# Values two slots behind their gates, and chain steps spread over the slots

## The chip, the cores and the metric

One core of a Trainium2 chip runs the whole program. The metric is the device time of one execution in microseconds (us). A profiled execution also has a span: the time from its first to its last instruction.

## The reference

The program is an attention block over 32 learned points, and then a gated feed-forward block. x has 4 batches of 12,416 tokens with 128 channels.

```
h   = softmax(scale * I @ x.T) @ x      # 32 x 128 for each batch
y   = softmax(scale * x @ h.T) @ h      # 12,416 x 128 for each batch
out = (relu(y @ w_gate) * (y @ w_val)) @ w_out
```

w_gate and w_val are 128 x 1,536, w_out is 1,536 x 128. Outputs are fp32.

## The kernel before, in words

y is never formed. h @ w_gate and h @ w_val are 32 x 1,536 and are kept as `hgv`, four blocks of 32 partitions (gate, value, gate, value). With p2, the unnormalised exponentials of the second softmax, a gate is p2 times a block of hgv: a matmul over 32 rows only. Gates and values for two blocks of 512 tokens use four different row groups of the TensorE array, so the four matmuls can run side by side. Both are off by the softmax sum, so the output is scaled by the square of its reciprocal at the end (z2i, twice in L498).

The main loop (L606 to L655) goes through slots. A pair is two blocks of 512 tokens; it has 12 slots, one for each 128 of the 1,536 columns. A batch has 12 pairs and then three small slots for the last 128 tokens: 147 slots, 588 in all. In a slot:

- TensorE forms the unit's two gates (L591, tile g_ps, one PSUM bank each, three banks with the tag "g") and, for the unit of the slot before, two values (v_ps, a tile of two banks, two tiles). The order is first gate, both values, second gate (L623 to L625).
- ScalarE writes Relu of the gates to g16 (L648, three buffers).
- VectorE multiplies g16 of the slot before with its values into gv (L651). This is the "multiply".
- TensorE does steps of jobs. A chain is 12 matmuls with w_out that add into the one "o" bank (L481), one for each slot of a pair; a pair has two chains, k = 0 and 1. ScalarE evicts a finished chain to oT (L487); a DMA on SyncE's queue transposes it; GpSimd scales it (L498); a DMA stores it. Other jobs: the softmax sums (z2, eight small matmuls for every second pair, then a reciprocal on VectorE), and in each of the first three batches the sums over tokens for the next batch's h (h_part, join).
- TensorE does fills: scores for the next pair (`ev_s2`, L164) and scores for the next batch (`s1`, L367). Each takes one of the three "g" banks, and ScalarE exponentiates it one slot later (L174; L377, tile p1T). hgv for the next batch is filled the same way (L143, L153).

`post[at]` holds work for other engines that is placed at the start of slot `at`: evictions, casts, transposes, loads, stores. The schedule is manual, so the order in the code is the order on each engine, and each engine works through its queue in that order.

Jobs go first come, first served. Each slot has a budget of 3; a chain step costs 1 and may run from its own slot on (`first + i`). When a job is done, the next may start two slots later (`free = at + 2`). Fills stand at fixed slots.

The next batch's x is loaded, cast on GpSimd, transposed by a DMA (L353, slot 16q + 11 of the batch) and scored (slot 16q + 20) while the present batch runs.

Of the kernel before, what the change touches and what calls it, by code (L numbers as in the profile page):

```python
# [2 lines left out]

# [7 lines left out]
FP16 = mybir.dt.float16  # L11
AF = mybir.ActivationFunctionType
ALU = mybir.AluOpType
# [4 lines left out]
def kernel(  # L18
# [133 lines left out]
    def hgv_evac(hgv, ps, k):  # L152
        nc.scalar.copy(out=hgv[:, k * BLK : (k + 1) * BLK], in_=ps)  # L153
# [117 lines left out]
    def slot(b, pr, s):  # L271
        return b * SPB + pr * NFF + s

    fill = defaultdict(list)
    post = defaultdict(list)

    def ev_s2(b, pr, at):
        def pe():
            s = state[b]
            ps = s2_pe(s["hT"], s["xT"], pr)  # L280

            def act():
                p2s[(b, pr)] = s2_exp(ps, pr)

            post[at + 1].append(act)

        fill[at].append(pe)

    jobs = []

    def job(steps, evac):
        jobs.append(dict(steps=steps, evac=evac))

    def ev_z2(b, pr):
        def pe():
            if pr < NPAIR:
                box["ps"] = z2_pe([p2s[(b, pr)], p2s[(b, pr + 1)]])
            else:  # L300
                box["ps"] = z2_rest_pe(p2s[(b, pr)])

        def dve(at):
            if pr < NPAIR:
                z2i = st([P, 2, TPB, 2], FP32, "z2i", 3)
                nc.vector.reciprocal(out=z2i, in_=box["ps"])
                z2is[(b, pr)] = z2i[:, 0, :, :]
                z2is[(b, pr + 1)] = z2i[:, 1, :, :]
            else:
                z2i = st([P, 1, 1], FP32, "z2r", 2)  # L310
                nc.vector.reciprocal(out=z2i[:, 0, :], in_=box["ps"])
                z2is[(b, pr)] = z2i

        box = {}
        base = slot(b, pr, 0)
        job([(base + (6 if pr < NPAIR else 0), 3, pe)], dve)

    for b in range(B):
        for pr in range(NPAIR + 1):
            if (b, pr) == (0, 0):  # L320
                pass
            elif pr == 0:
                ev_s2(b, 0, slot(b - 1, NPAIR - 1, 8))
            else:
                ev_s2(b, pr, slot(b, pr - 1, 3))


    def plan_phase1(b):
# [11 lines left out]
        for q in range(NCH):  # L340
            t0, t1 = crange(q)

            def load(q=q):
                s["x32", q] = load_x(b, q)

            def cast(q=q, t0=t0, t1=t1):
                nc.gpsimd.tensor_copy(  # L347
                    out=s["x16"][:, t0:t1, :], in_=s["x32", q]
                )

            def transp(q=q, t0=t0, t1=t1):
                s["xT"][q] = new_xT(q)
                nc.sync.dma_start_transpose(  # L353
                    out=s["xT"][q],
                    in_=s["x16"][:, t0:t1, :].rearrange("p t c -> p (t c)"),
                )

            at = at0 + 16 * q
            post[at + 3].append(load)
            post[at + 7].append(cast)  # L360
            post[at + 11].append(transp)

            def s1(q=q, at=at + 20):
                ps = bank("g", "s1T_ps")
                for r in range(4):
                    t = q * CT + r * TPB
                    nc.tensor.matmul(  # L367
                        ps[32 * r : 32 * r + 32, :],
                        indT,
                        xTs(s["xT"], t, TPB),  # L370
                        start=True,
                        stop=True,
                    )

                def act():
                    p1T = st([P, BLK], FP16, "p1T", 2)
                    nc.scalar.activation(  # L377
                        out=p1T, in_=ps, func=AF.Exp, scale=sm_scale, accum_out=s["zp"][:, q : q + 1]
                    )

                    def tr():
                        p1g = st([P, TPB, P], FP16, "p1g", NQ)
                        nc.sync.dma_start_transpose(out=p1g, in_=p1T)
                        s["p1g"][q] = p1g

                    post[at + 2].append(tr)

                post[at + 1].append(act)

            if q < NQ:  # L390
                fill[at + 20].append(s1)

        at = at0 + 16 * NQ + 16

        def s1_rest(at=at):
            ps = bank("g", "s1T_ps")
            nc.tensor.matmul(ps[0:M, 0:P], indT, xTs(s["xT"], NT - 1, 1), start=True, stop=True)

            def act():
                p1T = st([P, BLK], FP16, "p1T", 2)  # L400
                nc.scalar.activation(
                    out=p1T[0:M, 0:P],
                    in_=ps[0:M, 0:P],
                    func=AF.Exp,
                    scale=sm_scale,
                    accum_out=s["zp"][0:M, NQ : NQ + 1],
                )

                def tr():
                    p1r = st([P, 1, M], FP16, "p1r", 1)  # L410
                    nc.sync.dma_start_transpose(out=p1r, in_=p1T[0:M, 0:P])
                    s["p1r"] = p1r

                post[at + 2].append(tr)

            post[at + 1].append(act)

        fill[at].append(s1_rest)

        def h_part(q):  # L420
            if q == 0:
# [31 lines left out]
        def finish(at):  # L453
            s["hT"] = finish_h(s["hz_ps"][:, 0, :], s["hz_ps"][:, 1, :])
            s["hgv"] = new_hgv()
            for k in range(3):

                def mk(k=k, a=at + 2 + 2 * k):
                    ps = hgv_pe(s["hT"], k)
                    post[a + 1].append(lambda: hgv_evac(s["hgv"], ps, k))  # L460

                fill[at + 2 + 2 * k].append(mk)

        at = at0 + 16 * NQ + 19
        s["jobs"] = [
            ([(at, 2, lambda q=q: h_part(q)) for q in range(NQ + 1)], sums),
            ([(at, 2, join)], finish),
        ]

    for b in range(1, B):  # L470
# [3 lines left out]
    def chain(w, gv, key, k, t0, first):  # L474
# [10 lines left out]
        def evac(at):  # L485
# [29 lines left out]

            post[at + 1].append(tr)

        per = 1 if w == BLK else 4
        job(
            [(first + (i // per), 1 if w == BLK else 0.5, lambda i=i: step(i)) for i in range(NFF)],  # L520
            evac,
        )

    def units():
        for b in range(B):
            for pr in range(NPAIR + 1):
                base = slot(b, pr, 0)
                p2, hgv = p2s[(b, pr)], state[b]["hgv"]  # L530
                if pr < NPAIR:
# [7 lines left out]
                    for k in range(2):  # L539
                        chain(  # L540
                            BLK,
                            lambda i, k=k, gv=gv: gv(i, k),
                            (b, pr),
                            k,
                            (2 * pr + k) * TPB,
                            base + 2,
                        )
                    if b + 1 < B and pr == 8:
                        for j in state[b + 1]["jobs"]:
# [19 lines left out]
                else:  # L569
                    gvr = st([P, NFF, P], FP16, "gvr", 1)  # L570
                    ev_z2(b, pr)
                    chain(P, lambda i, g=gvr: g[:, i, :], (b, pr), 0, NT - 1, base + 2)
                    for s in range(3):
                        yield dict(
                            mm=[
# [27 lines left out]

        return gate

    free = 0  # L606
    at = 0
    todo_units = units()
    before = None
    while True:  # L610
        unit = next(todo_units, None)
        if not (unit or before or fill or post or jobs):
            break

        gs = []
        if unit:
            gate = gate_banks(unit)
            gs = [(gate, m) for m in unit["mm"][0]]
        vs = []
        if before:  # L620
            before["v"] = bank("v", "v_ps", [P, 2 * BLK])
            vs = [(lambda *m, ps=before["v"]: form(ps, *m), m) for m in before["mm"][1]]
        h = (len(gs) + 1) // 2  # L623
        for f, m in gs[:h] + vs + gs[h:]:
            f(*m)  # L625
        for f in post.pop(at, []):
            f()
        budget = 3.0 if unit else 100.0
        while jobs and free <= at and budget > 0:
            j = jobs[0]  # L630
            when, cost, f = j["steps"][0]
            if when > at:
                break
            f()
            budget -= cost
            j["steps"].pop(0)
            if not j["steps"]:
                jobs.pop(0)
                free = at + 2
                post[at + 1].append(lambda at=at, j=j: j["evac"](at + 1))  # L640
        for f in fill.pop(at, []):
            f()

        if unit:
            n = unit["dst"].shape[-1]
            g16 = unit["g16"] = st([P, 2 * BLK], FP16, "g16", 3)
            for k, ps in enumerate(unit["g"]):
                nc.scalar.activation(out=g16[:, k * BLK : (k + 1) * BLK], in_=ps, func=AF.Relu)  # L648
        if before:
            n = before["dst"].shape[-1]  # L650
            nc.vector.tensor_tensor(  # L651
                out=before["dst"], in0=before["g16"][:, 0:n], in1=before["v"][:, 0:n], op=ALU.mult
            )
        before = unit
        at += 1  # L655


# [28 lines left out]
```

## Time and profile before

| | |
|---|---|
| median of 3 runs | 806.71 us (802.96 to 806.79) |
| the profiled execution | 806.86 us, span 805.1 us, granted clock 0.901 |
| busy share of the span | TensorE 89%, ScalarE 88%, VectorE 87%, GpSimd 26% |
| VectorE multiplies (L651) | 576 of 128x1024, 674.4 us |
| ScalarE Relu (L648) | 616.3 us |
| chain matmuls (L481) | 354.0 us |

PE is TensorE's matmul row, PEld its weight loads, DVE VectorE, ACT ScalarE, POOL GpSimd, SP SyncE. Durations of neighbouring instructions can overlap by a part, so the distance from start to start says what one costs in a row of them. The granted clock is the share of full speed that TensorE was given. "Idle before <-X" names the instruction that ended an engine's idle time.

### The profile page before, as it was taken

How to read it: one execution, taken by the hardware profiler on the slowest of the kernel's cores; microseconds unless marked ns; L12 is line 12 of the kernel's file. 1: busy time of each engine (PE TensorE's matmuls, PEld its weight loads, DVE VectorE, ACT ScalarE, POOL GpSimd, SP SyncE). 2: the span in 40 equal slices, each digit the busy share in tenths (PEclk: the TensorE clock that was granted, in tenths of full speed). 3: DMA queues.
4: the chain of work that ended last, by engine and by line, in shares of the span. 5: the costliest groups of instructions: out<-in, count | busy, mean ns of one | idle time of the engine just before them, and what ended most of it. 6: DMA issues, size and time to landing. Idle time of an engine off the chain costs nothing.

```text
span 805.1 us, 13705 instructions
## 1 busy us (share of the span) xinstructions
PE 717.5 (89%) x4621; PEld 207.6 (26%) x4621; DVE 698.5 (87%) x666; ACT 707.2 (88%) x1390; POOL 207.6 (26%) x418
## 2 busy tenths in 40 slices
PE   5798898898999998989999999889899999998894
PEld 4422222222232222222222222222223222222221
DVE  3399999998998899899898988988899999898993
ACT  4589999998999899898898989998899999998993
POOL 0302332321232233322112333322122122212222
PEclk9779999998988899899897989998898899998998
DMA  8515555421154366441134547442112112121212
GB/s 312 185 24 144 125 144 149 137 55 35 50 149 127 106 146 155 114 96 55 27 103 132 143 102 168 112 122 54 35 50 71 43 46 73 47 60 40 59 54 63
DMA packets 121158, 78.76 MB, mean 98 GB/s; under 512 B 102880, under 2 KB 105472, under 8 KB 118016
## 3 DMA queue, kind: packets, MB, share of 16 engines
q1 hardware_dynamic: 121088, 77.89, 35.9%
q8 instruction: 36, 0.59, 0.3%
q14 instruction: 34, 0.28, 0.1%
HBM read 27.80 MB, written 25.43 MB: 66 GB/s over the span
## 4 chain that ended last, share of the span: by engine, by line
PE 56%; ACT 24%; issue 10%; DVE 8%; DMA 2%; POOL 0%; SPq 0%; POOLq 0%; ACTq 0%; DVEq 0%
PE o_ps L481 28%; PE g_ps L591 19%; ACT g L648 17%; DVE gv L651 8%; ACT oT L487 5%; PE v_ps L591 3%; PE s_ps L164 2%; DMA o<-oT 1%; PE xTb_ps L239 1%; DMA x<-in_x_dram 1%; PE h_ps L431 1%; PE hgv_ps L143 1%; ACT x L223 1%; PE s1T_ps L367 1%; ACT p L251 0%
## 5 line engine op out<-in xcount | busy, mean ns | idle before, releaser
L651 DVE TENSOR_TENSOR gv<-g,v_ps 128x1024 f16<-128x1024 f16 x576 | 674.4, 1214 | 68.7 <-PE g_ps L591 37.9
L648 ACT ACTIVATE g<-g_ps 128x512 f16<-128x512 f32 x1164 | 616.3, 621 | 45.2 <-PE g_ps L591 36.9
L481 PE MATMUL o_ps<-gv,wo 128*128 128x512 f16 x1152 | 354.0, 417 | 14.0 <-DVE gv L651 13.7
L591 PE MATMUL g_ps<-p,hgv 32*128 32x512 f16 (+1 forms) x1200 | 318.2, 401 | 41.8 <-ACT g L648 29.4
L498 POOL TENSOR_SCALAR osb<-o,z2i 128x128 f32<-128x128 f16 x384 | 166.2, 447 | 544.3 <-DMA o<-oT 361.5
L591 PE MATMUL v_ps<-p,hgv 32*128 32x512 f16 (+1 forms) x1200 | 245.2, 404 | 6.1 <-DVE gv L651 5.8
L591 PEld LDWEIGHTS <-hgv 32*128 32x128 f16 x2400 | 77.8, 92 | 281.0 <-issue 276.5
L481 PEld LDWEIGHTS <-wo 128*128 128x128 f16 x1200 | 90.3, 102 | 215.7 <-issue 176.8
L487 ACT CAST oT<-o_ps 128x512 f16<-128x512 f32 (+1 forms) x100 | 58.1, 581 | 4.0 <-PE o_ps L481 3.8
L174 ACT ACTIVATE p<-s_ps 128x512 f16<-128x512 f32 x48 | 29.1, 606 | 18.1 <-PE s_ps L164 16.0
L347 POOL CAST x<-x 128x2048 f16<-128x2048 f32 x18 | 34.0, 1889 | 10.7 <-DMA x<-in_x_dram 10.7
L164 PE MATMUL s_ps<-xT,hT 128*64 128x512 f16 x96 | 22.7, 468 | 2.1 <-DVE hT L137 1.6
L241 DVE COPY xT<-xT_ps 128x1024 f16<-128x1024 f16 x6 | 4.2, 692 | 14.5 <-PE xT_ps L239 14.5
L377 ACT ACTIVATE p1T<-s1T_ps 128x512 f16<-128x512 f32 x18 | 11.0, 614 | 2.8 <-PE s1T_ps L367 2.2
L164 PEld LDWEIGHTS <-hT 128*64 128x64 f16 x96 | 6.2, 112 | 25.9 <-issue 23.9
L243 ACT COPY xT<-xTb_ps 128x1024 f16<-128x1024 f16 x6 | 6.1, 1012 | 6.8 <-PE xTb_ps L239 6.8
L184 PEld LDWEIGHTS <-p 128*128 128x128 f16 x192 | 6.5, 97 | 21.4 <-issue 21.4
L239 PEld LDWEIGHTS <-x 128*128 128x128 f16 x97 | 9.1, 136 | 9.4 <-ACT x L223 5.3
L223 ACT CAST x<-x 128x1024 f16<-128x1024 f32 x6 | 6.2, 1038 | 4.3 <-DMA x<-in_x_dram 4.3
L239 PE MATMUL xT_ps<-eye,x 128*128 128x128 f16 x49 | 6.3, 305 | 3.9 <-DVE x L222 3.9
L153 ACT CAST hgv<-hgv_ps 128x512 f16<-128x512 f32 x12 | 6.9, 596 | 2.9 <-PE hgv_ps L143 2.7
L239 PE MATMUL xTb_ps<-eye,x 128*128 128x128 f16 x48 | 5.8, 295 | 4.1 <-ACT x L223 4.1
(75 smaller groups left out, 123.0 us busy)
## 6 DMA issues: line engine op xcount, KB each, us to landing
x<-in_x_dram SPq DMA_DIRECT2D x24, 1024.0 KB, 5.2
out_dram<-osb SPq DMA_DIRECT2D x96, 256.0 KB, 2.1
o<-oT SPq DMA_TRANSPOSE x100, 2.4
x<-in_moe_w_gate_dram SPq DMA_DIRECT2D x1, 768.0 KB, 4.0
x<-in_moe_w_val_dram SPq DMA_DIRECT2D x1, 768.0 KB, 4.3
x<-in_moe_w_out_dram SPq DMA_DIRECT2D x1, 768.0 KB, 5.9
xT<-x SPq DMA_TRANSPOSE x18, 4.3
p1g<-p1T SPq DMA_TRANSPOSE x18, 2.4
```

The source lines that it names most:

```text
L164: nc.tensor.matmul(ps[64 * k : 64 * k + 64, :], hT, xTs(xT, t0, TPB), start=True, stop=True)
L174: nc.scalar.activation(out=p2, in_=ps, func=AF.Exp, scale=sm_scale)
L223: nc.scalar.copy(out=x16[:, t0 + 8 : t1, :], in_=x32[:, 8:CT, :])
L239: nc.tensor.transpose(ps[:, t - a, :], x16[:, t, :], eye16)
L347: nc.gpsimd.tensor_copy(out=s["x16"][:, t0:t1, :], in_=s["x32", q])
L377: nc.scalar.activation(out=p1T, in_=ps, func=AF.Exp, scale=sm_scale, accum_out=s["zp"][:, q : q + 1])
L481: nc.tensor.matmul(c["ps"][:, 0:w], wo[:, i, :], gv(i), start=(i == 0), stop=(i == NFF - 1))
L487: nc.scalar.copy(out=oT[:, 0:w], in_=c["ps"][:, 0:w])
L498: nc.gpsimd.tensor_scalar(out=osb[:, t, :], in0=o16[:, t, :], scalar1=zz, scalar2=zz, op0=ALU.mult, op1=ALU.mult,)
L591: nc.tensor.matmul(ps[:, cols], hgv[:, s * P : (s + 1) * P], p2, start=True, stop=True)
L648: nc.scalar.activation(out=g16[:, k * BLK : (k + 1) * BLK], in_=ps, func=AF.Relu)
L651: nc.vector.tensor_tensor(out=before["dst"], in0=before["g16"][:, 0:n], in1=before["v"][:, 0:n], op=ALU.mult)
```

## The change

The jobs get a fixed number of steps for each of their slots, with one list for a job that starts on time and one for a job that starts late. The next job may start in the slot right after one ends. A chain of pair `base` starts from slot base + 10 (k = 0) and base + 16 (k = 1) on, not from base + 2. Fills get a first and a last slot; one fill is done in a slot without job steps, in a job's third slot, or when its last slot has come, and it stands ahead of the job's steps. Values are formed two slots behind their gates, ahead of both gates of the slot, and g16 has a fourth buffer.

```
+    def fill(first, last, f):
+        heapq.heappush(fills, (first, last, len(fills) + 1000 * first, f))
...
-        job([(base + (6 if pr < NPAIR else 0), 3, pe)], dve)
+        job([(base + (10 if pr < NPAIR else 0), pe)], dve, ([1], [1]))
...
-                ev_s2(b, 0, slot(b - 1, NPAIR - 1, 8))
+                a = slot(b - 1, NPAIR - 1, 0)
+                ev_s2(b, 0, a + 6, a + 11)
             else:
-                ev_s2(b, pr, slot(b, pr - 1, 3))
+                a = slot(b, pr - 1, 0)
+                ev_s2(b, pr, a + 1, a + (5 if pr == NPAIR else 8))
...
-                fill[at + 20].append(s1)
+                fill(at + 18, at + 26, s1)
...
-                fill[at + 2 + 2 * k].append(mk)
+                fill(at + 2, at + 7 + 3 * k, mk)
...
+            ([(at, lambda q=q: h_part(q)) for q in range(NQ + 1)], sums, ([1, 2, 2, 2],) * 2),
+            ([(at, join)], finish, ([1], [1])),
...
-        per = 1 if w == BLK else 4
-        job(
-            [(first + (i // per), 1 if w == BLK else 0.5, lambda i=i: step(i)) for i in range(NFF)],
-            evac,
-        )
+        if w == BLK:
+            steps = [(first if i == 0 else 0, lambda i=i: step(i)) for i in range(NFF)]
+            counts = ([1, 2, 1, 2, 3, 3], [1, 3, 2, 3, 3])
+        else:
+            steps = [(first + i // 4, lambda i=i: step(i)) for i in range(NFF)]
+            counts = ([4, 8], [4, 8])
+        job(steps, evac, counts)
...
-                            base + 2,
+                            base + 10 + 6 * k,
...
+    window = [None, None]
+    job_slot = 0
...
+        window.append(unit)
+        ready = window.pop(0)
...
+        if ready:
+            ready["v"] = bank("v", "v_ps", [P, 2 * BLK])
+            for m in ready["mm"][1]:
+                form(ready["v"], *m)
         if unit:
             gate = gate_banks(unit)
+            for m in unit["mm"][0]:
+                gate(*m)
...
+            if job_slot == 0 and j["steps"][0][0] <= at:
+                j["counts"] = j["counts"][1 if at > j["steps"][0][0] else 0]
+            if job_slot > 0 or j["steps"][0][0] <= at:
+                n_steps = j["counts"][job_slot] if job_slot < len(j["counts"]) else 3
+                job_slot += 1
+
+        if fills and fills[0][0] <= at:
+            if not n_steps or (job_slot == 3) or min(f[1] for f in fills) <= at:
+                heapq.heappop(fills)[3](at)
+        for _ in range(n_steps):
+            if j["steps"] and j["steps"][0][0] <= at:
+                j["steps"].pop(0)[1]()
...
-            g16 = unit["g16"] = st([P, 2 * BLK], FP16, "g16", 3)
+            g16 = unit["g16"] = st([P, 2 * BLK], FP16, "g16", 4)
...
-        if before:
-            n = before["dst"].shape[-1]
+        if ready:
+            n = ready["dst"].shape[-1]
             nc.vector.tensor_tensor(
-                out=before["dst"], in0=before["g16"][:, 0:n], in1=before["v"][:, 0:n], op=ALU.mult
+                out=ready["dst"], in0=ready["g16"][:, 0:n], in1=ready["v"][:, 0:n], op=ALU.mult
             )
```

## Rows read from the trace of the kernel before

**Rows 1.** The page's busy times, and the granted clock in 40 slices (tenths).

```profile
PE 717.5 (89%) x4621; PEld 207.6 (26%) x4621; DVE 698.5 (87%) x666; ACT 707.2 (88%) x1390; POOL 207.6 (26%) x418
...
PEclk9779999998988899899897989998898899998998
```

**Rows 2.** Busy time by stretch, the loop: all engines; then L651 alone (busy, count, clock).

```profile
38.80:792.60 753.80, 690.97 (x4284) 189.14 (x4283) 687.08 (x636) 686.35 (x1362) 196.16 (x399) 0.90 0.35 90
...
38.80:792.60 753.80, 682.00 (x588) 0.90 0.35 90
```

**Rows 3.** The waits of the whole execution: total us, times, longest us.

```profile
DVE gv L651 <- PE g_ps L591: 37.9, 92, 1.3
ACT g L648 <- PE g_ps L591: 36.9, 61, 1.1
PE g_ps L591 <- ACT g L648: 29.4, 86, 0.6
```

**Rows 4.** The timeline of TensorE's matmuls (start, us, instruction), half clock, then full.

```profile
301.32 0.60 PE L591 MATMUL g_ps<-p,hgv 32*128 32x512 f16 x1
...
303.26 0.60 PE L591 MATMUL g_ps<-p,hgv 32*128 32x512 f16 x1
...
309.93 0.39 PE L591 MATMUL g_ps<-p,hgv 32*128 32x512 f16 x1
...
310.26 0.82 PE L481 MATMUL o_ps<-gv,wo 128*128 128x512 f16 x3
311.01 0.38 PE L591 MATMUL g_ps<-p,hgv 32*128 32x512 f16 x1
```

**Rows 5.** The timeline of ScalarE, then of VectorE, from 311 us on.

```profile
311.43 1.09 ACT L648 ACTIVATE g<-g_ps 128x512 f16<-128x512 f32 x2
312.40 0.59 ACT L487 CAST oT<-o_ps 128x512 f16<-128x512 f32 x1
312.87 1.12 ACT L648 ACTIVATE g<-g_ps 128x512 f16<-128x512 f32 x2
313.83 0.65 ACT L377 ACTIVATE p1T<-s1T_ps 128x512 f16<-128x512 f32 x1
...
314.40 3.87 ACT L648 ACTIVATE g<-g_ps 128x512 f16<-128x512 f32 x7
...
315.63 3.48 DVE L651 TENSOR_TENSOR gv<-g,v_ps 128x1024 f16<-128x1024 f16 x3 [0.34 <-PE g_ps L591]
```

**Rows 6.** The timeline of VectorE: two runs of multiplies without a break.

```profile
41.03 4.60 DVE L651 TENSOR_TENSOR gv<-g,v_ps 128x1024 f16<-128x1024 f16 x4
...
88.86 13.98 DVE L651 TENSOR_TENSOR gv<-g,v_ps 128x1024 f16<-128x1024 f16 x12 [0.24 <-PE g_ps L591]
```

**Rows 7.** L651 by stretch: sums of the 25 half-clock, then 25 full-clock stretches.

```profile
sum 132.90, DVE 101.91; mean DVE 4.08
...
sum 590.70, DVE 552.29; mean DVE 22.09
```

**Rows 8.** Chain matmuls by stretch: 3 us before 25 falls; full clock otherwise.

```profile
sum 75.00, PE 7.55; mean PE 0.30
...
sum 503.20, PE 254.14; mean PE 10.17
```

**Rows 9.** The timeline of TensorE around the clock's fall at 79.0 us.

```profile
74.96 0.82 PE L481 MATMUL o_ps<-gv,wo 128*128 128x512 f16 x3
...
77.48 0.35 PE L184 MATMUL z_ps<-sel,p 128*128 128x2 f16 x8
...
79.65 0.61 PE L481 MATMUL o_ps<-gv,wo 128*128 128x512 f16 x1
```

**Rows 10.** The tile xT: time from issue to landing of its DMA transposes.

```profile
DMA to landing us min/median/max: 4.3/4.3/6.3
```

**Rows 11.** The timeline around the last multiplies.

```profile
790.27 0.68 DVE L651 TENSOR_TENSOR gvr<-g,v_ps 128x512 f16<-128x512 f16 x1
790.40 0.38 PE L481 MATMUL o_ps<-gv,wo 128*128 128x512 f16 x1 [0.42 <-DVE gv L651]
```

More of the change, by code (lines that the diff above doesn't have):

```diff
@@ L1 @@
+import heapq
 from collections import defaultdict
@@ L272, in slot, with ev_s2, pe @@
         return b * SPB + pr * NFF + s
-    fill = defaultdict(list)
+    fills = []
     post = defaultdict(list)
-    def ev_s2(b, pr, at):
-        def pe():
+    def fill(first, last, f):
+        heapq.heappush(fills, (first, last, len(fills) + 1000 * first, f))
+    def ev_s2(b, pr, first, last):
+        def pe(at):
             s = state[b]
@@ L285, in pe, with job @@
             post[at + 1].append(act)
-        fill[at].append(pe)
+        fill(first, last, pe)
     jobs = []
-    def job(steps, evac):
-        jobs.append(dict(steps=steps, evac=evac))
+    def job(steps, evac, counts):
+        jobs.append(dict(steps=steps, evac=evac, counts=counts))
     def ev_z2(b, pr):
@@ L361, in plan_phase1, with s1 @@
             post[at + 11].append(transp)
-            def s1(q=q, at=at + 20):
+            def s1(at, q=q):
                 ps = bank("g", "s1T_ps")
@@ L390, in plan_phase1, with s1_rest @@
             if q < NQ:
-                fill[at + 20].append(s1)
+                fill(at + 18, at + 26, s1)
         at = at0 + 16 * NQ + 16
-        def s1_rest(at=at):
+        def s1_rest(at):
             ps = bank("g", "s1T_ps")
@@ L416, in s1_rest @@
             post[at + 1].append(act)
-        fill[at].append(s1_rest)
+        fill(at, at + 6, s1_rest)
         def h_part(q):
@@ L456, in finish, with mk @@
             for k in range(3):
-                def mk(k=k, a=at + 2 + 2 * k):
+                def mk(at, k=k):
                     ps = hgv_pe(s["hT"], k)
-                    post[a + 1].append(lambda: hgv_evac(s["hgv"], ps, k))
-                fill[at + 2 + 2 * k].append(mk)
+                    post[at + 1].append(lambda: hgv_evac(s["hgv"], ps, k))
+                fill(at + 2, at + 7 + 3 * k, mk)
         at = at0 + 16 * NQ + 19
         s["jobs"] = [
-            ([(at, 2, lambda q=q: h_part(q)) for q in range(NQ + 1)], sums),
-            ([(at, 2, join)], finish),
+            ([(at, lambda q=q: h_part(q)) for q in range(NQ + 1)], sums, ([1, 2, 2, 2],) * 2),
+            ([(at, join)], finish, ([1], [1])),
         ]
@@ L571, in units @@
                     ev_z2(b, pr)
-                    chain(P, lambda i, g=gvr: g[:, i, :], (b, pr), 0, NT - 1, base + 2)
+                    chain(P, lambda i, g=gvr: g[:, i, :], (b, pr), 0, NT - 1, base + 4)
                     for s in range(3):
@@ L604, in gate_banks @@
         return gate
-    free = 0
     at = 0
     todo_units = units()
-    before = None
+    window = [None, None]
+    job_slot = 0
     while True:
         unit = next(todo_units, None)
-        if not (unit or before or fill or post or jobs):
+        window.append(unit)
+        ready = window.pop(0)
+        if not (unit or any(window) or ready or fills or post or jobs):
             break
-        gs = []
+        if ready:
+            ready["v"] = bank("v", "v_ps", [P, 2 * BLK])
+            for m in ready["mm"][1]:
+                form(ready["v"], *m)
@@ L616 @@
         if unit:
             gate = gate_banks(unit)
-            gs = [(gate, m) for m in unit["mm"][0]]
-        vs = []
-        if before:
[L621 to L625, printed above, removed]
+            for m in unit["mm"][0]:
+                gate(*m)
         for f in post.pop(at, []):
             f()
-        budget = 3.0 if unit else 100.0
@@ L629 @@
-        while jobs and free <= at and budget > 0:
+        n_steps = 0
+        if jobs:
             j = jobs[0]
[L631 to L642, printed above, removed]
+            if job_slot == 0 and j["steps"][0][0] <= at:
[3 more added lines that the diff above has]
+                job_slot += 1
@@ L644 @@
+        if fills and fills[0][0] <= at:
[4 more added lines that the diff above has]
+                j["steps"].pop(0)[1]()
+        if n_steps and not j["steps"]:
+            jobs.pop(0)
+            job_slot = 0
+            post[at + 1].append(lambda at=at, j=j: j["evac"](at + 1))
         if unit:
-            n = unit["dst"].shape[-1]
@@ L646 @@
-            g16 = unit["g16"] = st([P, 2 * BLK], FP16, "g16", 3)
+            g16 = unit["g16"] = st([P, 2 * BLK], FP16, "g16", 4)
             for k, ps in enumerate(unit["g"]):
                 nc.scalar.activation(out=g16[:, k * BLK : (k + 1) * BLK], in_=ps, func=AF.Relu)
-        if before:
-            n = before["dst"].shape[-1]
+        if ready:
+            n = ready["dst"].shape[-1]
             nc.vector.tensor_tensor(
-                out=before["dst"], in0=before["g16"][:, 0:n], in1=before["v"][:, 0:n], op=ALU.mult
+                out=ready["dst"], in0=ready["g16"][:, 0:n], in1=ready["v"][:, 0:n], op=ALU.mult
@@ L653 @@
             )
-        before = unit
         at += 1
```

## The prediction

> **What bounds the kernel now.** I read the page first. VectorE, ScalarE and TensorE are each busy for 87 to 89% of the span, all the way through, and the granted clock is below full in nearly every slice [rows 1]. No engine is the bound by itself, so the question is what keeps three nearly equal engines from overlapping. The loop runs from the first multiply at 38.8 us to the end of the last at 792.6 us: 588 slots in 753.8 us, with VectorE idle for 66.7 us of it and ScalarE for 67.5 us [rows 2]. The other 53.1 us of the execution's 806.9 us lie before and after. 576 multiplies are full ones, 12 (three in each batch) small.
>
> The waits say who holds whom: VectorE and ScalarE both wait longest for TensorE (37.9 and 36.9 us), and TensorE in turn for ScalarE to empty a gate bank (29.4 us) [rows 3]. The reader should see a ring, not one slow engine.
>
> Next, what one slot needs on each engine. TensorE: a slot with three chain matmuls takes 1.08 us at full clock (309.93 to 311.01) and 1.94 us at half (301.32 to 303.26) [rows 4]. The three stream one after another, 0.82 us with the last one's 0.39 us, so 0.215 us each; the four gate and value matmuls with what surrounds them are the remaining 0.43 us. Two steps would need about 0.86 us, one 0.65 us (estimates from these rows). ScalarE: two Relus take 0.97 us (311.43 to 312.40, and 0.96 us from 312.87), a chain's eviction 0.47 us, a p1T exponential with its accumulator 0.57 us [rows 5]. VectorE: twelve multiplies in a row took 13.98 us, 1.165 us each, and a shorter run of four 1.13 us each after the first ((4.60 - 1.21)/3) [rows 6].
>
> So over a pair of 12 slots ScalarE needs 12 x 0.97 + 2 x 0.47, one score exponential and a quarter of an hgv eviction (priced like a chain's, 0.6 together) and 0.3 for half a p1T: 13.5 us. VectorE needs 13.6 to 14.0. They are equal on average but not slot by slot: a slot with an eviction costs ScalarE 1.44, one without 0.97. To average out, ScalarE must get ahead in the short slots. It can't, for two reasons. Slots that carry chain work carry three steps, and TensorE then delivers gates every 1.08 us. And the second gate of slot s is queued behind values s-1, which need the bank that multiply s-3 frees. The rows show the price: ScalarE works without a break through an eviction and a p1T, the gates behind them come late, and VectorE, which has no finished slot in hand, stands idle 0.34 us at 315.63 [rows 5].
>
> The clock is the second loss. The granted clock is either 1.00 (2.4 GHz) or 0.50 (1.2 GHz). I compared the 25 stretches at half clock after 60 us with those at full clock: multiplies keep VectorE busy for 101.91 of 132.9 us there (0.767) and 552.29 of 590.7 us (0.935) otherwise [rows 7]. That costs 132.9 x (1 - 0.767/0.935) = 24 us. Each fall follows a drought of chain matmuls: in the 3 us before the 25 falls TensorE spent 7.55 of 75 us on them, never more than three matmuls; in the full-clock time farther from a fall it is 254.14 of 503.2 us [rows 8]. At 76 us the drought is an empty slot, the sums and another empty slot: no chain matmul between the three from 74.96 and the one at 79.65, by then at half clock [rows 9].
>
> Without the clock loss and about 10 us for the 12 small multiplies (0.69 us each [rows 11] and some wait), a full slot costs (753.8 - 24 - 10)/576 = 1.25 us.
>
> **The change part by part.**
>
> *Even steps.* Counting the slots by the code: before, a chain is four slots of three steps and an empty one. Of the 588 slots 367 hold three steps and 179 none. After, two pairs run as sums, 1,3,2,3,3, then three chains of 1,2,1,2,3,3: 228 slots with three, 151 with two, 151 with one, 52 with none. Runs of three neighbouring slots with at most three steps together fall from 115 to 15, mainly at the starts and ends of batches. By the rows a stretch filled this way did not lose its clock. I leave a quarter of the 24 us, as handovers stretch some slots: 6 us remain (bounds 0 and 24). The work itself is the same: 1,200 chain matmuls, the same evictions, transposes and stores at the same offsets behind each chain.
>
> *The clock, against a rule.* The rows put falls after chain droughts, not after brief waits. The Trainium skill (TensorE: Matmul & The Clock Gate, section "A second HAM failure mode: psum-queue depth-cycling") says that short idles between groups of matmuls, bank after bank, are enough to make the clock swing. By that rule the even plan, which idles a little in every slot, would keep falling and the sum would be some 18 us more; the rows of the full-clock stretches, with waits in nearly every slot, do not show it.
>
> *Values two slots late, fourth g16.* Values of s-2 now lead slot s and wait only for multiply s-4, and the gates of s for the same. ScalarE may thus run one slot, 1.13 us or more, farther ahead. An eviction costs it 0.3 us against VectorE and a short slot gives back 0.16, so one slot of lead covers an eviction, an exponential and part of a p1T together. With two steps on average, TensorE's 0.86 us lets ScalarE run at its own 0.97. I take 1.165 us for a full slot, VectorE's own longest run in this trace, with bounds of 1.13 (its shortest spacing) and 1.20 (half the idle left).
>
> *Chains back to back.* The empty slot after a chain goes. The next chain's first step needs the single o bank, so TensorE waits for the eviction, which ScalarE runs between two slots. Behind that step stand the next slot's values and gates. With ScalarE a slot ahead this is hidden: those values wait for VectorE's bank anyway. Without that cover it is the slower rival below. The sums and the chain after them wait likewise for a reciprocal on VectorE. I cost both at nothing, bound by the rival.
>
> *More switches between gate tiles and full matmuls.* 536 slots instead of 409 have both kinds. The 0.43 us beside three steps holds two 0.215 us, so at most 0.22 us for the turn: 127 x 0.22 = 28 us of TensorE. TensorE needs about 11 us of a pair's 14, so VectorE hides it; uncovered, in half-clock stretches, it is part of the 6 us.
>
> *Moved fills.* Scores for the next batch come up to two slots earlier, from slot 18 on instead of at 20, seven slots after the transpose of x is issued at slot 11. Seven slots are 8.2 us; the slowest transpose landed 6.3 us after issue [rows 10]. Hidden, 1.9 us to spare, unless its cast is late on GpSimd; SP's queue keeps its order of loads, transposes and stores. The sums move from slot 6 to 10, behind the score exponential and still ahead of the scale that reads them. A fill goes ahead of chain steps in its slot and into a light slot, same matmuls: nothing.
>
> *Ends.* The first values come after both gates of slot 1: 0.5 us. At the end, one step of the last pair's first chain (0.38 us) was left when its last multiply released it [rows 11]; now six remain then, so five times 0.215, about 1 us, more.
>
> **Sum** for the profiled execution: 576 x 1.165 = 671, small multiplies 10, clock 6, outside 53.1 + 1.5 = 54.6: 742 us, 65 less than 806.9. That execution is within 0.2 us of the median, 806.7, so the same number stands for it.
>
> **Rivals.**
> 1. *The clock goes on falling*, because even slots still carry only a few steps. For it: the 1,2,1 slots hold four steps, near the three that came before falls. Against it: the full-clock rows. Then 24 us remain, 742 + 18 = 760 us. That is also what the Trainium skill's rule above would make of it.
> 2. *The extra slot of lead is not used*, since gates still share three banks with scores and fills, so that TensorE still waits for ScalarE in order (29.4 us now). The change would then do only half of what it says: 1.25 us a slot and the clock gain, 806.9 - 18 + 1.5 = 790 us.
> 3. *Slower: the eviction wait.* Where VectorE runs right on ScalarE's heels, multiply s-2 starts 0.97 + 0.47 us before the eviction ends and is done 0.3 us before it; the next values come only after the waiting step (0.215), the start (0.1) and their own 0.43, 0.75 us after it. VectorE idles 1.05 us. At all 96 chains that is 101 us: 843 us. It decides from 62 chains on (65/1.05), if ScalarE's lead is under 0.75 us at each. Against it: the stall itself makes VectorE late and rebuilds the lead.
> 4. *No difference*, 807 us: gains and eviction waits cancel.
>
> **Chances.** The forecast 0.62, rival 1 0.18, rival 2 0.09, rival 3 0.07, rival 4 0.04. Faster by over 0.5% (4 us, about what a measurement of this kernel can tell from no change) is 0.89, within it 0.04, slower 0.07. The forecast's own range is 721 (1.13 us, all the clock back) to 768 (1.20 us and a quarter of the clock loss); rival 1 ends inside it. I give 720 to 785, which leaves out rivals 2 to 4.
>
> **What would show it.** Right: multiplies about 1.165 us apart; VectorE's wait for TensorE at a third or less; far fewer than 25 half-clock stretches; TensorE's waits moved from gates to o_ps behind oT and to v_ps behind VectorE, harmless. Wrong: o_ps waiting for oT followed at once by VectorE waiting for v_ps (rival 3); as many falls, now after 1,2,1 slots (rival 1); ScalarE still waiting some 30 us for gates with VectorE idle at full clock (rival 2); scores held by a transpose.

## The result, and the profile after

The changed kernel takes 760.0 us (759.48 to 761.18), 0.946 of the time before, with a 95% interval of 0.939 to 0.953. The forecast was 742 us, with 720 to 785. The profiled execution took 759.48 us. Its page, to be set beside [rows 1]:

```profile
span 757.7 us, 13705 instructions
PE 656.5 (87%) x4621; PEld 194.7 (26%) x4621; DVE 692.7 (91%) x666; ACT 695.3 (92%) x1390; POOL 208.5 (28%) x418
PEclk9759999999999999999999999999999999999997
L663 DVE TENSOR_TENSOR gv<-g,v_ps 128x1024 f16<-128x1024 f16 x576 | 668.3, 1213 | 25.8 <-PE g_ps L601 19.4
```

The work is the same, instruction for instruction in number; the clock row is what looks different. From the stretches of the loop, first all engines, then the multiplies (line 663 now) in the half-clock stretches after 60 us, to be set beside [rows 2] and [rows 7] (length, then busy and count of each engine or of the line, then the granted clock):

```profile
38.90:743.10 704.20, 630.02 (x4276) 177.39 (x4273) 681.28 (x635) 673.07 (x1360) 197.51 (x399) 0.98 0.38 96
...
sum 20.50, DVE 14.47; mean DVE 2.41
```

The loop takes 704.2 us instead of 753.8, and 55.3 us lie outside it instead of 53.1. Of the 25 half-clock stretches with 132.9 us, 6 with 20.5 us are left. The waits answer to [rows 3] (us in total, times, longest):

```profile
PE o_ps L489 <- ACT oT L495: 40.4, 69, 0.6
...
DVE gv L663 <- PE g_ps L601: 19.4, 36, 5.2
ACT g L660 <- PE g_ps L601: 19.3, 42, 1.0
```

TensorE's wait for gate banks, 29.4 us before, is no longer among the larger ones; in its place stands the forecast wait of a chain's first step for the eviction. VectorE's and ScalarE's waits for TensorE are halved; a third or less was the forecast for VectorE's. So far this is the forecast's picture in the main. Which part of the change did it, the experiments had to say, and there the forecast was wrong.

### The profile page after: what moved, and what is told of

Same layout as the page of the kernel before. It is cut to its first block, busy times and chain, and to the rows that moved or that the text cites. A ratio compares the mean times of both kernels' runs of the same rounds, so it can differ in the third digit from the quotient of the medians.

```text
span 757.7 us, 13705 instructions
## 1 busy us (share of the span) xinstructions
PE 656.5 (87%) x4621; PEld 194.7 (26%) x4621; DVE 692.7 (91%) x666; ACT 695.3 (92%) x1390; POOL 208.5 (28%) x418
## 4 chain that ended last, share of the span: by engine, by line
PE 53%; ACT 24%; issue 14%; DVE 7%; DMA 1%; POOL 0%; SPq 0%; POOLq 0%; DVEq 0%; ACTq 0%
PE o_ps L489 25%; ACT g L660 15%; PE v_ps L601 15%; PE g_ps L601 7%; DVE gv L663 6%; ACT oT L495 6%; PE s_ps L165 3%; PE xTb_ps L240 1%; PE s1T_ps L375 1%; DMA x<-in_x_dram 1%; ACT x L224 1%; DMA o<-oT 1%; PE z_ps L185 1%; ACT xT L244 1%; DVE z2i L312 1%
## 5 line engine op out<-in xcount | busy, mean ns | idle before, releaser
L660 ACT ACTIVATE g<-g_ps 128x512 f16<-128x512 f32 x1164 | 612.3, 616 | 29.4 <-PE g_ps L601 19.3
L489 PE MATMUL o_ps<-gv,wo 128*128 128x512 f16 x1152 | 346.4, 389 | 47.8 <-ACT oT L495 40.4
L601 PE MATMUL g_ps<-p,hgv 32*128 32x512 f16 (+1 forms) x1200 | 297.7, 381 | 1.8
L601 PE MATMUL v_ps<-p,hgv 32*128 32x512 f16 (+1 forms) x1200 | 232.8, 385 | 3.8 <-DVE gv L663 2.8
L489 PEld LDWEIGHTS <-wo 128*128 128x128 f16 x1200 | 84.5, 97 | 209.5 <-issue 179.7
L601 PEld LDWEIGHTS <-hgv 32*128 32x128 f16 x2400 | 65.5, 91 | 268.8 <-issue 263.4
L355 POOL CAST x<-x 128x2048 f16<-128x2048 f32 x18 | 34.1, 1894 | 13.6 <-DMA x<-in_x_dram 13.6
L185 PE MATMUL z_ps<-sel,p 128*128 128x2 f16 x192 | 8.1, 163 | 8.1 <-ACT oT L495 7.4
L165 PEld LDWEIGHTS <-hT 128*64 128x64 f16 x96 | 9.3, 110 | 19.8 <-issue 15.5
L663 DVE TENSOR_TENSOR gvr<-g,v_ps 128x512 f16<-128x512 f16 x12 | 8.2, 685 | 2.0 <-PE g_ps L601 1.2
```

The lines of the kernel that those rows point to most:

```text
L165: nc.tensor.matmul(ps[64 * k : 64 * k + 64, :], hT, xTs(xT, t0, TPB), start=True, stop=True)
L185: nc.tensor.matmul(ps[:, j, t, :], p2[:, t * P : (t + 1) * P], sel, start=True, stop=True)
L355: nc.gpsimd.tensor_copy(out=s["x16"][:, t0:t1, :], in_=s["x32", q])
L489: nc.tensor.matmul(c["ps"][:, 0:w], wo[:, i, :], gv(i), start=(i == 0), stop=(i == NFF - 1))
L601: nc.tensor.matmul(ps[:, cols], hgv[:, s * P : (s + 1) * P], p2, start=True, stop=True)
L663: nc.vector.tensor_tensor(out=ready["dst"], in0=ready["g16"][:, 0:n], in1=ready["v"][:, 0:n], op=ALU.mult)
```

## The experiments

Times are medians; the ratio is to the kernel before on the same chip, where it took 804.84 us beside the change and 806.31 to 806.74 beside the others. "Loop" and "clock" are length and mean granted clock of the stretch from the first multiply to the end of the last, in the profiled execution; "half clock" is the number of half-clock stretches after 60 us in it, and the time that they take.

| kernel | us | ratio (95%) | loop | clock | half clock, us |
|---|---|---|---|---|---|
| before | 804.84 | | 753.8 | 0.90 | 25, 132.9 |
| the change | 760.0 | 0.946 (0.939 to 0.953) | 704.2 | 0.98 | 6, 20.5 |
| even steps alone | 760.73 | 0.946 (0.937 to 0.954) | 705.0 | 0.97 | 7, 27.3 |
| lag alone | 810.13 | 1.007 (1.002 to 1.011) | 757.4 | 0.90 | 26, 131.3 |
| a gap behind chains | 780.14 | 0.969 (0.961 to 0.977) | 726.1 | 0.94 | 17, 71.7 |
| no handover | 744.0 | 0.925 (0.919 to 0.932) | 687.9 | 0.99 | 1, 3.4 |
| before, fills moved | 798.78 | 0.990 (0.987 to 0.994) | 746.9 | 0.92 | 24, 112.6 |
| the change, old fills | 757.2 | 0.938 (0.935 to 0.942) | 702.7 | 0.98 | 2, 13.7 |
| flat steps | 766.68 | 0.949 (0.946 to 0.952) | 709.6 | 0.97 | 10, 34.1 |
| the change, old order | 756.51 | 0.937 (0.934 to 0.941) | 699.9 | 0.97 | 4, 20.5 |
| before, clock held | 772.91 | 0.959 (0.957 to 0.960) | 719.2 | 1.00 | 0 |
| its control | 805.31 | 0.999 (0.995 to 1.002) | 746.4 | 0.92 | 25, 110.9 |
| old order and old fills | 758.4 | 0.940 (0.939 to 0.942) | 702.6 | 0.97 | 4, 20.5 |
| the same, join later | 755.93 | 0.938 (0.936 to 0.940) | 699.6 | 0.98 | 4, 13.7 |

### Even steps alone, lag alone

Even steps alone, in the changed kernel:

```
-    window = [None, None]
+    window = [None]
...
+        for f, m in gs[:h] + vs + gs[h:]:
+            f(*m)
...
-            g16 = unit["g16"] = st([P, 2 * BLK], FP16, "g16", 4)
+            g16 = unit["g16"] = st([P, 2 * BLK], FP16, "g16", 3)
```

> Only the even steps, back-to-back chains and movable fills; values stay one slot behind their gates, in the old order, with three g16. Theory A (the clock comes from the even steps, the smoothing from the second slot of lag): under 10 half-clock stretches, but a pair stays near 14.5 us, as at full clock before; 775 to 785 us. Theory B (the second slot of lag does all of it): about as slow as before, 795 to 810. Theory C (without the lag the eviction waits are uncovered and cost about 1 us at a chain): over 810 us.

760.73 us: as fast as the whole change. Lag alone, in the kernel before:

```
+    window = [None, None]
...
+        window.append(unit)
+        before = window.pop(0)
...
-                            base + 2,
+                            base + 3,
...
-            g16 = unit["g16"] = st([P, 2 * BLK], FP16, "g16", 3)
+            g16 = unit["g16"] = st([P, 2 * BLK], FP16, "g16", 4)
```

with the values ahead of both gates, as in the change.

> Only the values two slots behind, ahead of the gates, with a fourth g16; jobs and fills as before (chains may start one slot later, base + 3, because their products come a slot later). Theory A: the clock falls about as often as before (20 or more stretches), so most of its 24 us stays, and TensorE's three-step slots of 1.08 us keep ScalarE from getting ahead: 785 to 797 us. Theory B: 760 to 770 us, as with the whole change.

810.13 us, no gain and by the interval a little slower. Its waits:

```profile
DVE gv L650 <- PE g_ps L591: 63.4, 103, 1.5
ACT g L647 <- PE g_ps L591: 53.8, 73, 1.4
```

VectorE waits for TensorE 63.4 us instead of the 37.9 before, and the granted clock is 0.90 as before. The expectations that gave the lag a part failed: its part is nothing that these runs can tell from zero, with uneven steps or with even ones. In both runs the lag goes with the new order in the slot and the fourth buffer; the old order is looked at by itself below.

### Is it the wait for the eviction?

```
-            counts = ([1, 2, 1, 2, 3, 3], [1, 3, 2, 3, 3])
+            counts = ([2, 2, 2, 3, 3], [1, 3, 2, 3, 3])
```

> The whole change, but a chain that starts on time takes five slots (2,2,2,3,3), so that an empty slot lies between it and the next one, and the eviction is not waited for there. Theory A (the eviction waits are hidden): TensorE's 40 us of waiting for oT fall to a third and the time stays at 756 to 765 us. Rival (the waits are where the 18 us beyond the forecast went): 740 to 750 us.

```profile
ACT g L660 <- PE g_ps L601: 38.3, 69, 0.9
DVE gv L663 <- PE g_ps L601: 38.2, 93, 5.2
PE o_ps L489 <- ACT oT L495: 18.6, 33, 0.6
```

TensorE's wait for oT falls from 40.4 to 18.6 us, to about a half, and the kernel is 20 us slower: the clock is down to 0.94, with 17 half-clock stretches in place of 6, and ScalarE and VectorE wait for TensorE as long as before the change. At the price of half-clock time worked out below (39.5 us for 132.9), the 51 us more of it are some 15 of the 20 us (an estimate). So the empty slot costs more than the wait that it saves, most of it by the clock; the first slot of a chain holds two steps here and not one, which was not tried apart. Both theories had the sign or the size wrong.

How such a wait stays hidden is seen in the changed kernel's timeline at a chain's end (start, us, instruction):

```profile
248.73 2.34 DVE L663 TENSOR_TENSOR gv<-g,v_ps 128x1024 f16<-128x1024 f16 x2
...
249.32 0.59 ACT L495 CAST oT<-o_ps 128x512 f16<-128x512 f32 x1
...
249.97 0.38 PE L489 MATMUL o_ps<-gv,wo 128*128 128x512 f16 x1 [0.59 <-ACT oT L495]
...
250.28 0.39 PE L601 MATMUL v_ps<-p,hgv 32*128 32x512 f16 x2
```

TensorE stands for 0.59 us, the values come at 250.28, and VectorE works on without a gap until 251.07.

### The clock by itself

The kernel before with two extra full matmuls at the end of every slot without chain steps; they go into the value bank that the next slot overwrites:

```
+        if unit and not chain_steps:
+            unit["v"] = bank("v", "v_ps", [P, 2 * BLK])
+            for k in range(2):
+                nc.tensor.matmul(
+                    unit["v"][:, k * BLK : k * BLK + 512], wo[:, k, :], wo[:, 0:TPB, :], start=True, stop=True
+                )
```

> The kernel before, plan unchanged, with two extra full matmuls of 512 columns in each slot that holds no chain step; they are written into the value bank that the next slot overwrites, so the output stays. They add some 360 matmuls to TensorE and take no work away. Theory K (nearly all of the gain of the even steps is the clock, whose loss of 24 us in the prediction was sized too small): the clock hardly falls, and the time is 760 to 775 us although TensorE has more to do. Theory P (the clock is worth about 24 us, the rest comes from the shape of the plan): 783 us or more with few falls.

The control has the same edit with 32 columns in place of 512.

> The same as the run with the extra matmuls, but they have 32 columns each: the same waits and order, hardly any work. Theory K: the clock falls as often as before and the time is 800 to 815 us. If the extra instructions or the earlier wait for the value bank help by themselves: under 790 us.

The loops, first with 512 columns:

```profile
39.40:758.60 719.20, 662.22 (x4649) 196.15 (x4648) 686.50 (x636) 692.64 (x1362) 197.54 (x399) 1.00 0.39 95
```

and the control:

```profile
38.10:784.50 746.40, 664.70 (x4649) 203.35 (x4649) 686.90 (x636) 688.50 (x1362) 197.54 (x399) 0.92 0.36 91
```

Both have 365 more matmuls than the loop of [rows 2] (x4649, x4284). With 512 columns the clock does not fall once in the loop, which takes 34.6 us less than before; with 32 columns it falls as before, and the time is not to be told from the kernel before. So useless work on TensorE, with the old plan and the old order, brings 33 us (806.31 to 772.91), where the change brought 45. This is the clock, not the shape of the plan and not the extra instructions.

The timeline of the run with 512 columns, at the place of [rows 9]:

```profile
75.82 0.59 PE L649 MATMUL v_ps<-wo 128*128 128x512 f16 x2 [0.34 <-DVE gv L660]
...
76.84 0.35 PE L184 MATMUL z_ps<-sel,p 128*128 128x2 f16 x8
77.06 0.59 PE L649 MATMUL v_ps<-wo 128*128 128x512 f16 x2
```

### What else: fills, flat steps, order

Fills moved, in the kernel before: the heap of the change, but a fill goes into a slot in which no job step can run, or in its last slot.

```
+        busy = jobs and free <= at and jobs[0]["steps"][0][0] <= at
+        if fills and fills[0][0] <= at and (not busy or min(f[1] for f in fills) <= at):
+            heapq.heappop(fills)[3](at)
         while jobs and free <= at and budget > 0:
```

> The kernel before with its greedy jobs; only the fills are movable and go into a slot without job steps, ahead of steps otherwise. Theory F (a score in a three-step slot is what made slots at full clock long: 1.08 us of TensorE and some 0.4 more in one slot): 785 to 795 us, with about as many half-clock stretches as before. Theory E (the runs of three-step and empty slots do it): 800 to 810 us.

798.78 us, 1% faster: between the two expectations, nearer to theory E. The other way round, in the changed kernel:

```
-                ev_s2(b, pr, a + 1, a + (5 if pr == NPAIR else 8))
+                ev_s2(b, pr, a + 3, a + 3)
...
-                fill(at + 18, at + 26, s1)
+                fill(at + 20, at + 20, s1)
...
+        while fills and fills[0][0] <= at:
+            heapq.heappop(fills)[3](at)
```

> The whole change, but the fills stand at the old fixed slots, behind the slot's job steps, which in the new plan is mostly a slot with three steps. Theory F: half of the gain at full clock is lost, 772 to 785 us. Theory E: 757 to 766 us, as with the whole change.

757.2 us: moving the fills is worth nothing once the steps are even. Flat steps:

```
-            counts = ([1, 2, 1, 2, 3, 3], [1, 3, 2, 3, 3])
+            counts = ([2, 2, 2, 2, 2, 2], [2, 2, 2, 3, 3])
```

> The whole change with two steps in every slot of a chain that starts on time (2,2,2,2,2,2), and 2,2,2,3,3 for a late one, in place of 1,2,1,2,3,3 and 1,3,2,3,3. Theory E (three-step slots are long): as fast or some us faster, 750 to 760 us. Theory L (the light first slot matters, since the first step waits for the eviction and a second one behind it pushes the next values back): slower, 765 to 775 us.

766.68 us, 7 us slower than the whole change and, beside the two changed kernels run with it on the same chip, some 10 slower; there are ten half-clock stretches in place of six, which is some 4 us at the price used above (an estimate). Theory L had the range, but whether the wait behind the first step makes the rest was not shown. Old order, in the changed kernel, with the second slot of lag kept:

```
+        for f, m in gs[:h] + vs + gs[h:]:
+            f(*m)
```

> The whole change, values still two slots behind their gates and four g16, but in the old order in the slot: first gate, both values, second gate. The run with even steps alone came to 760.7 us, the whole change to 760.0. If the second slot of lag is worth something that the new order takes away: 748 to 755 us. If neither does anything here: 757 to 764 us.

756.51 us, at the edge of both. The new order may cost the few us that the lag gives; 3.5 us between kernels that ran on different chips is too little to say so.

### The handover between batches

Without the sums over tokens, the join and the hgv fills of the later batches:

```
-                        for j in state[b + 1]["jobs"]:
-                            job(*j)
+                        state[b + 1]["hT"] = state[0]["hT"]
+                        state[b + 1]["hgv"] = state[0]["hgv"]
```

> The whole change without the sums over tokens, the join and the hgv fills of the later batches; all batches use the first batch's h. Theory A (the 18 us beyond the forecast lie in the handover between batches, where pairs 9 to 11 take 46.4 us instead of 41.3, and in the fills of next-batch scores): about 15 us less, 742 to 748 us. Rival (they lie in ordinary slots): 754 us or more.

744.0 us: 16 us less, as expected. This run leaves out the handover's work together with its waits. In the changed kernel, pairs of 12 slots by stretch: pairs 2 and 3 of the second batch, its pairs 9, 10 and 11, and pair 9 of the last batch, which prepares nothing (multiplies at the edges are counted twice):

```profile
247.60:261.30 13.70, 13.61 (x13) 1.00 0.60 159
261.30:275.60 14.30, 14.07 (x14) 1.00 0.51 115
346.50:361.40 14.90, 14.04 (x13) 1.00 0.20 56
361.40:377.50 16.10, 14.27 (x13) 0.89 0.14 42
377.50:392.90 15.40, 14.28 (x12) 1.00 0.24 60
699.20:713.10 13.90, 13.76 (x12) 1.00 0.20 58
```

An ordinary pair takes 13.7 us, 1.14 a slot, with VectorE hardly ever idle; a pair with a fill of next-batch scores some 0.6 more; the handover's three pairs 46.4 us instead of 41. The timeline at 361 us shows how:

```profile
361.12 0.41 PE L458 MATMUL hz_ps<-stackI,hp 128*128 128x32 f32 x2 [0.78 <-DVE hp L449]
...
361.37 1.22 DVE L663 TENSOR_TENSOR gv<-g,v_ps 128x1024 f16<-128x1024 f16 x1
...
362.31 1.09 ACT L660 ACTIVATE g<-g_ps 128x512 f16<-128x512 f32 x2 [0.93 <-PE g_ps L601]
...
363.12 0.38 PE L489 MATMUL o_ps<-gv,wo 128*128 128x512 f16 x1 [0.88 <-DVE hT L137]
```

TensorE waits for VectorE's copy of the sums (0.78 us), then for hT (0.88 us), each of which stands behind a multiply; ScalarE runs dry (0.93 us); and the clock falls at 364.2 us. The other two handovers show the same two waits, each with a fall behind it (at 186.7 and 541.7 us): three of the six falls. The last run tried to part the two waits. With the old order and the old fills:

> The whole change with the gates and values in the old order and the fills at their old slots behind the steps; each alone came out some 3 us under the whole change. If they add up: 750 to 754 us; if they are the same few us: 755 to 758 us.

758.4 us: the few us do not add up. On top of it, the join behind the first chain of pair 9:

```
+                        if b + 1 < B and pr == 9 and k == 0:
+                            job(*state[b + 1]["jobs"][1])
                     if b + 1 < B and pr == 8:
-                        for j in state[b + 1]["jobs"]:
-                            job(*j)
+                        job(*state[b + 1]["jobs"][0])
```

> The same as the run with old order and old fills, but the join for the next batch stands behind the first chain of pair 9, five slots after the sums over tokens, so that TensorE does not wait for VectorE's copies right there. Theory A (the handover costs some 15 us, mostly two waits for VectorE in a row, the lost lead and a fall of the clock): 5 to 9 us less than that run, 744 to 750 us. If the cost is the added work alone: within 2 us of it.

755.93 us, 2.5 less where 5 to 9 were expected; the intervals overlap. But the two waits are still there. Of the waits from 530 to 550 us, around the third handover:

```profile
PE o_ps L489 <- DVE hp L449: 0.9, 1, 0.9
...
PE o_ps L489 <- DVE hT L137: 0.6, 1, 0.6
```

The sums, the join and the chains share the one "o" bank, so the chain step that now follows the sums waits for VectorE's copy in the join's place. The run parts the waits and hardly shortens them, so it does not say what the handover would cost without them: of its 16 us, the shares of the work, of the waits and of the falls stay open. The versions between 755.9 and 760.7 us are not clearly apart from one another.

## Why the prediction was right, and where it was not

**The ring of waits and the droughts** were read rightly as to what helps: with even steps the falls go from 25 to 6. A quarter of the clock loss was left in the forecast; of the half-clock time, 20.5 of 132.9 us stayed.

**The clock term was mis-sized**: 24 us lost before, 18 to be regained. Holding the clock gave 34.6 us in the loop, with extra matmuls to pay for. The step that failed is the price of a half-clock stretch, which was taken from VectorE's busy share inside these stretches alone [rows 7]. The engines wait on after a stretch: of the 37.9 us that VectorE waited for TensorE [rows 3], 12.0 lie in the 25 stretches and 15.9 in the 6 us behind them. The multiplies of the kernel before in the 6 us after each of the 25 rises, then in the full-clock time that lies neither there nor in the 4 us before a fall:

```profile
sum 150.00, DVE 131.01; mean DVE 5.24
...
sum 329.70, DVE 315.00; mean DVE 14.32
```

The share is 0.873 just after a rise and 0.955 elsewhere. Against 0.955 the stretches cost 132.9 x (1 - 0.767/0.955) = 26 us and what follows them 150 x (1 - 0.873/0.955) = 13 us: 39 us, near the 34.6 measured with extra work on board.

The held run settles where it lies. From the end of one multiply to the end of the next, slot for slot, the kernel before is slower than the held run by 24.2 us in the slots of the 25 stretches and by 15.3 us in those of the 6 us behind them, 39.5 us in all, and 4.8 us quicker in all others, which the extra matmuls make longer. The control, which has the held run's instructions one for one, is slower than it by 20.7 and 12.4 us in the same two places. So 24 us was right for the stretches themselves; what the prediction put at nothing is the time behind them.

**The lag term was wrong in its cause.** The forecast gave the full slot 49 us, from 1.25 to 1.165 us, for the second slot of lag and the even steps together, and said that gates behind values kept ScalarE from getting ahead. The lag alone gave nothing, and without it even steps gave all. What the full slots gained belongs to the even steps: from the held clock's 719.2 us to the change's 704.2 us, and about 5 us more for the 20.5 us still at half clock (34.6 x 20.5/132.9), some 20 us at most, less what the extra matmuls cost, about 5 us by the slots counted above: about 15 us. How these split between the end of three-step runs, of empty slots and of chains that wait for their own products was not separated; moving the fills back in the changed kernel cost nothing.

**A slot of 1.165 us** holds for ordinary pairs (1.14 to 1.19) and was too good for a mean, (704.2 - 10 - 5)/576 = 1.197: the best run of VectorE was laid over every slot, the three handovers too. Their pairs 9 to 11 take 47.2, 46.5 and 47.0 us, where 36 slots of 1.165 are 41.9: some 15 of the 18 us between the two means. Without the handover's work the kernel takes 744.0 us, 2 us over the forecast.

**The total came near in part by luck**: the gain by the clock was put at 18 us and is some 33 (39.5 less 6 for what stayed), the gain by the slots was put at 49 us and is some 15, and the two errors partly cancel. The forecast's own range does not follow from its words either: 1.13 us a slot with all the clock back is 576 x 1.13 + 10 + 54.6 = 716 us, not 721, and 1.20 us with a quarter of the clock loss is 762, not 768.

**The ends** cost 2.2 us against 1.5. **The moved scores** are not held by their transposes: no wait for xT stands among the changed kernel's larger ones. **The turns between gate tiles and full matmuls** do not hold VectorE up in an ordinary pair, where it is busy for 13.61 of 13.70 us; elsewhere this was not shown.

**The rivals.** The clock did not go on falling as before (rival 1): 6 stretches are left of 25, and that the measured time is rival 1's 760 us is chance. TensorE waits 69 times for an eviction, 40.4 us in all, with the clock at 0.98. The Trainium skill (TensorE: Matmul & The Clock Gate, section "A second HAM failure mode: psum-queue depth-cycling") tells of a kernel whose clock swings because TensorE idles a little, often, between groups of matmuls. By that the even plan should have kept falling, and this case's trace does not agree. The prediction's argument against it, waits in nearly every slot at full clock, was put too strongly: in the kernel before TensorE stood idle for over 0.05 us in 233 of 464 such slots. Rival 2 was right in its first half, the lag buys nothing, and wrong in its price, since the even steps carry the slots too. Rival 3 did not come: the waits for the eviction are there, 0.59 us each, and where the timeline was read VectorE had work in hand.

## What to carry to other kernels

Price a clock fall by what comes after it too, and test the price by holding the clock up with work that nobody reads, beside a control with as many instructions and little work. Where chains of full matmuls share TensorE with small-row tiles, try to spread the chains' steps over all slots; here a short wait in a busy slot was cheaper than an empty slot. When two edits have one story, predict each alone: here one of them carried everything.

## What the runs showed of the hardware

TensorE can be busy most of the time by the profile and lose its clock. All engines in the 3 us before the fall at 79.0 us, and the sum over the 25 falls:

```profile
76.00:79.00 3.00, 2.47 (x23) 0.81 (x19) 2.89 (x5) 3.00 (x8) 1.73 (x4) 1.00 0.08 29
...
sum 75.00, PE 62.34 PEld 19.19 DVE 73.30 ACT 73.50 POOL 21.89; mean PE 2.49 PEld 0.77 DVE 2.93 ACT 2.94 POOL 0.88
```

TensorE was busy for 62.34 of the 75 us (0.83, against 0.91 in the full-clock time of [rows 8]), with no wait above 0.43 us, and full chain matmuls were 7.55 us of it. From 76 us to the fall it formed gates and values, matmuls over 32 rows, and the sums, matmuls with two columns, at clock 1.00 until it fell to 0.50; beside [rows 9]:

```profile
77.17 0.37 PE L591 MATMUL g_ps<-p,hgv 32*128 32x512 f16 x1 [0.33 <-ACT g L648]
...
77.76 0.39 PE L591 MATMUL v_ps<-p,hgv 32*128 32x512 f16 x2
```

Two matmuls of 128 rows and 512 columns in such a slot kept the clock at 1.00 from 41.4 us to the end of the loop at 758.6; two of 32 columns did not. As the full ones also fill idle time, whether the kind of matmuls or the idle time decides stays open. The 365 extra matmuls made a kernel 33 us faster whose TensorE was already busy for 89% of the span.

A stretch at half clock costs time after its end as well: 24.2 us in 132.9 us at half clock, and 15.3 us more in the 6 us behind each.
